# The last pair of token blocks as seven half-size products instead of eight, with its own order, its own bank for the last 128 tokens, and stores by column halves

## The chip, the cores and the metric

The kernel runs on one core of a Trainium2 chip. PE is the matrix engine (PEld its weight loads), DVE the vector engine, ACT the scalar engine, SP the engine that issues most of the DMAs; PSUM is the memory into which PE writes. The metric is the device time of one execution in microseconds (us). Most executions of one kernel lie within 0.4 us of each other; some take 1 to 2 us more. I therefore quote medians. For what happens at the end of the kernel I use a finer measure, the **tail**: the time from the start of the last hidden-layer eviction (the last ACT ReLU of 128x1024) to the end of the span. The start of the kernel, which varies from run to run, does not enter it. Times written like +10.21 are counted from that ReLU. Each tail is of the one execution of a kernel that was profiled.

## The reference

```python
def _attn_ref(x, f_logit, lower_bound):          # x: 4 x 6144 x 256
    sig = 1.0 / (1.0 + np.exp(-f_logit))
    f = lower_bound + (1.0 - lower_bound) * sig
    h = 0
    for t in range(S):                            # gated recurrence over the sequence
        h = f[:, t] * h + (1.0 - f[:, t]) * x[:, t]
        y[:, t] = h
    return y

def _moe_ref(x, w1, w2, w_out):                   # x: 24576 x 256, d_ff 1024
    g = np.maximum(x @ w1, x @ w2)
    return (g @ w_out).astype(np.float32)
```

## The kernel before

Tokens come in 48 blocks of 512. The kernel computes `max(h1, h2) = h1 + relu(h2 - h1)`, so that the second layer is `relu(y @ wd) @ w_out + y @ w13`: ten matmuls per 128 tokens, eight on hidden units and two on `y`. The hidden units and `y` are cut into two halves (`k` = 0, 1) and the 256 output columns too (`lo`, `hi`). Two blocks `ja`, `jb` make a pair, and for all pairs but some first ones and **the last** the second layer is done by a scheme of seven products instead of eight (`sevenths`). Sums of activations (`sum1` to `sum4`, on DVE) and of weights (`t1` to `t4`, made once) go in; PSUM banks X, E and B collect the products. The products of one pair run in the gaps of the next pair's first layer:

```python
        product("X", part(0, 0), plain(0, lo), True)   # M1
        then(seed("B", "X"))                           # ACT copies X into bank B
        product("E", sub(1), given(t1), True)          # M5
        then(snapshot("E", 5))                         # ACT copies E to SBUF
        product("X", sub(2), given(t2))                # M6
        then(snapshot("X", 2))
        product("B", part(0, 1), plain(1, lo))         # M2
        then(leave("B", ja, lo, None, False))          # ACT:  ja lo = B
        product("X", sub(3), given(t3))                # M7
        then(leave("X", jb, hi, 5, False))             # DVE:  jb hi = X + M5
        product("E", sub(4), plain(1, hi))             # M3
        then(leave("E", ja, hi, 2, True))              # DVE:  ja hi = E + (M1 + M6); store ja
        product("X", part(1, 1), given(t4))            # M4
        then(leave("X", jb, lo, None, True))           # ACT:  jb lo = X; store jb
```

Each product is 20 matmuls of 128x128 weights by 128 columns. The last pair has no next pair to hide behind, so it was done the plain way, with 40 matmuls of 256 columns per block, and the last block was evicted and stored in four quarters of 128 KB:

```python
        for step in queue:
            step()
        for j in (NBLK - 2, NBLK - 1):
            for slot in range(FC):
                second_layer(j, slot)
    # ... in second_layer:
            if j == NBLK - 1 and s == n - 1:
                (nc.vector.tensor_copy if r else nc.scalar.copy)(
                    out=osb[:, i : i + 1, :], in_=ps[:, r : r + 1, :]
                )
                store(j, osb, i, 1, nc.sync if r else nc.scalar)
```

Of the kernel before, what the change touches and what calls it, by code (L numbers as in the profile page):

```python
# [14 lines left out]
P = 128  # L15
# [3 lines left out]
def kernel(  # L19
# [429 lines left out]
                func=AF.Relu,  # L449
            )  # L450

    def store(j, osb, first=0, n=TB // P, queue=None):
        b, t0, nb, c, o = blocks[j]
        r0 = b * S + t0
        (queue or nc.sync).dma_start(
            out=out[r0 : r0 + nb, :].rearrange("(p n) d -> p n d", p=P)[
                :, first : first + n, :
            ],
            in_=osb[:, first : first + n, :],
        )  # L460

    acc = {}
# [1 line left out]
    def second_layer(j, slot):  # L464
        ns = TB // P
        n = KC + FC
        total = ns * n
        for k in range(slot * total // FC, (slot + 1) * total // FC):
            i, s = divmod(k, n)
            g, r = divmod(i, 2)  # L470
            if s == 0 and (r == 0 or j == NBLK - 1):
                acc["ps"] = ps_o.tile([P, 2, D], FP32, name="ps")
                if i == 0:
                    acc["osb"] = opool.tile([P, TB // P, D], FP32, name="osb")
            ps, osb = acc["ps"], acc["osb"]
            toks = slice(i * P, (i + 1) * P)
            if s < KC:
                left, right = y_of(j, s)[:, i:TB:ns], w13[:, s, :]
            else:
                fc = s - KC  # L480
                left, right = rts[j, fc // KH][:, fc % KH, toks], wob[:, fc, :]
            nc.tensor.matmul(  # L482
                ps[:, r, :],
                lhsT=left,
                rhs=right,
                start=(s == 0 and (r == 0 or j == NBLK - 1)),
                stop=(s == n - 1 and (r == 1 or j == NBLK - 1)),
                skip_group_check=True,
            )
            if j == NBLK - 1 and s == n - 1:  # L490
                (nc.vector.tensor_copy if r else nc.scalar.copy)(
                    out=osb[:, i : i + 1, :], in_=ps[:, r : r + 1, :]
                )
                store(j, osb, i, 1, nc.sync if r else nc.scalar)
            elif r == 1 and s == n - 1:
                (nc.scalar.copy if j == 0 else nc.vector.tensor_copy)(  # L496
                    out=osb[:, 2 * g : 2 * g + 2, :], in_=ps[:]
                )
                if i == ns - 1:
                    store(j, osb)  # L500
# [11 lines left out]
    def sum3(p):  # L512
        sum_of(p, 3, quarter(p, 0, 0), quarter(p, 1, 0), ALU.subtract)

    def sum2(p):
        sum_of(p, 2, quarter(p, 1, 1), sums[p, 3][:], ALU.subtract)

    def sum1(p):
        sum_of(p, 1, quarter(p, 1, 0), quarter(p, 1, 1), ALU.add)
# [4 lines left out]
    def sevenths(p):  # L524

        bank, snap, osbs = {}, {}, {}
        steps = []
        ja, jb = 2 * p, 2 * p + 1

        def product(b, left, w, fresh=False):  # L530
            for i in range(TB // P):
                for k in range(KH + 1):
                    steps.append([b, left, w(k), i, k, fresh and i == k == 0, None])

        def then(fn):
            steps[-1][-1] = fn

        def open_bank(b):
            bank[b] = ps_o.tile([P, TB // P, P], FP32, name="ps")

        def seed(b, src):
            def go():
                open_bank(b)
                nc.scalar.copy(out=bank[b][:], in_=bank[src][:])
            return go

        def snapshot(b, name):
            def go():
                t = snpool.tile([P, TB // P, P], FP32, name="sn")
                nc.scalar.copy(out=t[:], in_=bank[b][:])  # L550
                snap[name] = t
            return go

        def leave(b, j, cols, name, last):
            def go():
                if j not in osbs:
                    osbs[j] = opool.tile([P, TB // P, D], FP32, name="osb")
                dst = osbs[j][:, :, cols]
                if name is None:
                    nc.scalar.copy(out=dst, in_=bank[b][:])  # L560
                else:
                    nc.vector.tensor_tensor(  # L562
                        out=dst, in0=bank[b][:], in1=snap[name][:], op=ALU.add
                    )
                if last:
                    store(j, osbs[j])
            return go

        def sub(n):
            return lambda: sums[p, n]  # L570

        def part(t, k2):
            return lambda: rts[2 * p + t, k2]

        def plain(k2, cols):
            a, b = right(k2, cols)
            return lambda k: a[:, k, :] if k < KH else b

        def given(t):
            return lambda k: t[:, k, :]  # L580

        product("X", part(0, 0), plain(0, lo), True)
        then(seed("B", "X"))
        product("E", sub(1), given(t1), True)
        then(snapshot("E", 5))
        product("X", sub(2), given(t2))
        then(snapshot("X", 2))
        product("B", part(0, 1), plain(1, lo))
        then(leave("B", ja, lo, None, False))
        product("X", sub(3), given(t3))  # L590
        then(leave("X", jb, hi, 5, False))
        product("E", sub(4), plain(1, hi))
        then(leave("E", ja, hi, 2, True))
        product("X", part(1, 1), given(t4))
        then(leave("X", jb, lo, None, True))

        def runner(step):
            b, left, w, i, k, fresh, after = step

            def run():  # L600
                if fresh:
                    open_bank(b)
                a = left()
                cols = slice(i * P, (i + 1) * P) if k < KH else slice(i, TB, TB // P)
                nc.tensor.matmul(  # L605
                    bank[b][:, i, :],
                    lhsT=a[:, k, cols],
                    rhs=w,
                    start=fresh,
                    stop=after is not None,  # L610
                    skip_group_check=True,
                )
                if after is not None:
                    after()
            return run

        return [runner(s) for s in steps]

    with tc.manual_schedule():
# [93 lines left out]
        for p in range(PAIR0, NPAIR):  # L713
            first = p == PAIR0
            more = p + 1 < NPAIR
            seq = [(27, scans[p]["scan10"]), (36, scans[p]["scan11"])]
            if more:
                scans[p + 1] = pair_scans(p + 1)
                seq += [
                    (64, scans[p + 1]["decay0"]),  # L720
                    (66, scans[p + 1]["drive0"]),
                    (70, scans[p + 1]["scan00"]),
                    (84, scans[p + 1]["scan01"]),
                    (112, lambda: sum3(p)),
                    (131, scans[p + 1]["decay1"]),
                    (133, scans[p + 1]["drive1"]),
                ]
            if not first:
                seq += [
                    (9, lambda: sum1(p - 1)),  # L730
                    (18, lambda: sum2(p - 1)),
                    (50, lambda: sum4(p - 1)),
                ]
                queue += sevenths(p - 1)
            seq.sort(key=lambda e: e[0])
            gates = {4: 0, 6: 1, 12: 2, 14: 3} if more else {}
            for slot in range(2 * FC):
                first_layer(2 * p + slot // FC, slot % FC)
                if first and slot % 2:
                    second_layer(2 * p - 1, slot // 2)  # L740
                if p > PAIR0 + 1 or (p == PAIR0 + 1 and slot >= LAG):
                    due += NSEV / (2 * FC)
                    while due >= 1:
                        due -= 1
                        queue.pop(0)()
                if slot == 2 and p + 3 < NPAIR:
                    cross(blocks[2 * p + 6][3])
                if slot in gates:
                    pair_gate(p + 1, gates[slot])
                while seq and seq[0][0] < (slot + 1) * 9:  # L750
                    seq.pop(0)[1]()
        for step in queue:
            step()
        for j in (NBLK - 2, NBLK - 1):
            for slot in range(FC):
                second_layer(j, slot)


# [28 lines left out]
```

## Time and profile before

| kernel before | |
|---|---|
| time, median of 3 runs | 380.85 us (380.81 to 381.16) |
| span of the profiled run | 379.8 us |
| tail (last ReLU to end) | 14.37 us |
| last matmul ends | +10.21 |
| last eviction ends | +10.66 |
| last store issued / last packet done / landed | +10.69 / +12.04 / +12.60 |

The page of the kernel before, its span, the busy times and the clock that was granted to TensorE in 40 slices:

```profile
span 379.8 us, 9454 instructions
...
PE 369.1 (97%) x4076; PEld 279.9 (74%) x4076; DVE 333.0 (88%) x402; ACT 300.3 (79%) x406; POOL 37.5 (10%) x79
...
PEclk9999999999999999999999999999999999999999
```

PE is busy for 97% at the full clock; the body of the kernel is bound by it. The chain that ended last, before, in order of time, its last two pieces (start, length, what):

```profile
365.36 1.51 PE ps L605 x27
366.87 8.75 PE ps L482 x80
```

The chain leads through 80 matmuls of L482, the second layer of the last pair, 8.75 us. The timeline of the same stretch (start, length, engine, line, operation, result and operands, count, idle time before):

```profile
365.40 1.02 ACT L444 ACTIVATE r<-dT 128x1024 f16<-128x1024 f32 x1 [0.79 <-PE dT L436]
...
365.54 1.17 PEld L605 LDWEIGHTS <-r 128*128 128x128 f16 x20
...
366.65 8.67 PEld L482 LDWEIGHTS <-r 128*128 128x128 f16 x80
...
374.57 1.04 PE L482 MATMUL ps<-wob,r 128*128 128x256 f16 x8
...
375.64 0.42 DVE L491 COPY osb<-ps 128x256 f32<-128x256 f32 x1 [1.76 <-PE ps L482]
```

Here one reads the two cadences that the change trades: 80 weight loads and matmuls of 256 columns in 8.75 us, 109 ns each, and just before them 20 of 128 columns from 365.54 to 366.65, 55.5 ns each. Before its last copy DVE sat idle for 1.76 us, waiting for PE. The DMA view of the last 6.4 us before (373.4 to 379.8; one digit is 0.16 us, the mean busy share of the 16 DMA engines in tenths):

```profile
DMA  9999699249810008950000895000000000000100
...
out_dram<-osb SPq DMA_DIRECT2D x2, 128.0 KB, 1.9
out_dram<-osb ACTq DMA_DIRECT2D x1, 128.0 KB, 1.8
```

The last two stores land 1.8 to 1.9 us after their issue.

### The profile page before, as it was taken

To read this page: it belongs to the slowest core of one execution; us is meant where nothing else is said; L and a number is where in the kernel's file an instruction comes from. 1 tells how busy PE (TensorE), PEld (TensorE's weight loads), DVE (VectorE), ACT (ScalarE), POOL (GpSimd) and SP (SyncE) were. 2 spreads that over 40 slices of the span, in tenths; PEclk is the share of its full clock that TensorE was granted. 3 is DMA by queue.
4 is the path that set the end of the run, shared out by engine and by line. 5 is a ranking of instruction groups with operands and counts; after the bars stand their busy time and mean duration, and the time that the engine had idled before them with its cause. 6 is when DMAs were issued, how large, how long until landed. Compare 5 with 4: busy or idle time off the path is not lost.

```text
span 379.8 us, 9454 instructions
## 1 busy us (share of the span) xinstructions
PE 369.1 (97%) x4076; PEld 279.9 (74%) x4076; DVE 333.0 (88%) x402; ACT 300.3 (79%) x406; POOL 37.5 (10%) x79
## 2 busy tenths in 40 slices
PE   4999999999999999999999999999999999999995
PEld 3677766777777777777777777777777777777784
DVE  4696789999999999999999999999999999999721
ACT  4846788798798888888888887987888888888740
POOL 1500103101201101102011011011011021000000
PEclk9999999999999999999999999999999999999999
DMA  7994999989999999999899999999999999970223
GB/s 249 242 226 98 265 162 256 167 156 289 195 195 276 180 190 251 202 172 285 143 257 190 219 251 278 127 263 223 182 263 212 188 268 211 192 265 3 110 113 113
DMA packets 103389, 77.17 MB, mean 203 GB/s; under 512 B 93554, under 2 KB 94066, under 8 KB 102642
## 3 DMA queue, kind: packets, MB, share of 16 engines
q1 hardware_dynamic: 100514, 51.13, 59.8%
q0 software_dynamic: 2544, 25.17, 34.5%
q8 instruction: 32, 0.52, 0.6%
q10 hardware_dynamic: 288, 0.26, 0.2%
q14 instruction: 11, 0.09, 0.1%
HBM read 53.48 MB, written 48.23 MB: 268 GB/s over the span
## 4 chain that ended last, share of the span: by engine, by line
PE 89%; DMA 4%; DVE 3%; POOL 1%; SPq 1%; ACT 0%; issue 0%
PE ps L605 42%; PE dT L436 41%; PE ps L482 6%; DMA xT<-in_x_dram 3%; DMA r<-in_moe_w_dram 1%; DVE r L230 1%; DVE S L506 1%; SPq L117 0%; PE ps L180 0%; DVE osb L496 0%; DVE v L223 0%; POOL fT L105 0%; DVE ff L213 0%; ACT r L444 0%; POOL wob L631 0%
## 5 line engine op out<-in xcount | busy, mean ns | idle before, releaser
L444 ACT ACTIVATE r<-dT 128x1024 f16<-128x1024 f32 x192 | 195.8, 1022 | 53.2 <-PE dT L436 53.0
L436 PE MATMUL dT<-r,wd 128*128 128x512 f16 x768 | 225.4, 379 | 1.0 <-DVE wd L360 0.5
L605 PEld LDWEIGHTS <-S 128*128 128x128 f16 x1680 | 110.9, 101 | 37.6 <-issue 0.6
L605 PEld LDWEIGHTS <-r 128*128 128x128 f16 x1260 | 87.3, 101 | 36.6
L230 DVE TENSOR_TENSOR_SCAN r<-ff,r,v 128x512 f16<-128x512 f16 x88 | 108.2, 1270 | 0.8
L605 PE MATMUL ps<-t,S 128*128 128x128 f16 x1260 | 97.8, 219 | 0.0
L436 PEld LDWEIGHTS <-wd 128*128 128x128 f16 x768 | 67.6, 113 | 6.4 <-DVE wd L360 1.1
L506 DVE TENSOR_TENSOR S<-r 128x2560 f16<-128x2560 f16 x42 | 62.4, 1485 | 10.1 <-ACT r L444 10.0
L605 PE MATMUL ps<-wob,r 128*128 128x128 f16 x672 | 67.4, 219 | 0.0
L506 DVE TENSOR_TENSOR S<-r,S 128x2560 f16<-128x2560 f16 x42 | 61.9, 1474 | 0.0
L285 ACT ACTIVATE u<-fT 128x512 f16<-128x512 f16 x88 | 56.0, 636 | 1.0 <-DMA fT<-scr 1.0
L213 DVE TENSOR_SCALAR ff<-u,nom 128x512 f16<-128x512 f16 (+1 forms) x98 | 31.3, 346 | 9.7 <-ACT u L207 5.3
L348 POOL CAST waited<-fT 128x1 f32<-128x1 f16 x21 | 10.8, 513 | 279.5 <-DMA fT<-scr 279.5
L605 PE MATMUL ps<-w,r 128*128 128x128 f16 x168 | 36.8, 219 | 0.0
L562 DVE TENSOR_TENSOR osb<-ps,sn 128x512 f32<-128x512 f32 x42 | 28.7, 684 | 6.8 <-ACT osb L560 5.3
L605 PE MATMUL ps<-t,r 128*128 128x128 f16 x420 | 33.4, 219 | 0.0
L605 PE MATMUL ps<-wob,S 128*128 128x128 f16 x336 | 31.4, 219 | 0.0
L223 DVE TENSOR_TENSOR v<-u,xT 128x1024 f16<-128x1024 f16 x44 | 30.1, 684 | 0.2 <-DMA xT<-scr 0.2
L482 PEld LDWEIGHTS <-r 128*128 128x128 f16 x240 | 23.9, 101 | 6.9
L482 PE MATMUL ps<-wob,r 128*128 128x256 f16 x192 | 26.8, 273 | 0.0
L550 ACT COPY sn<-ps 128x512 f32<-128x512 f32 x42 | 24.6, 587 | 1.1 <-PE ps L605 0.9
L560 ACT COPY osb<-ps 128x512 f32<-128x512 f32 x42 | 24.4, 582 | 0.5 <-PE ps L605 0.5
(56 smaller groups left out, 134.8 us busy)
## 6 DMA issues: line engine op xcount, KB each, us to landing
out_dram<-osb SPq DMA_DIRECT2D x47, 512.0 KB, 3.9
scr<-in_f_logit_dram POOLq DMA_DIRECT2D x22, 512.0 KB, 7.4
scr<-in_x_dram POOLq DMA_DIRECT2D x22, 512.0 KB, 10.4
r<-in_moe_w_dram SPq DMA_DIRECT2D x4, 512.0 KB, 6.8
fT<-in_f_logit_dram POOLq DMA_DIRECT2D x3, 256.0 KB, 9.2
xT<-in_x_dram POOLq DMA_DIRECT2D x3, 256.0 KB, 11.1
osb<-in_f_logit_dram SPq DMA_DIRECT2D x2, 256.0 KB, 4.5
osb<-in_x_dram SPq DMA_DIRECT2D x2, 256.0 KB, 4.1
```

Of the source, the lines that this page charges most:

```text
L213: nc.vector.tensor_scalar(out=ff[:, h, cols], in0=u[:, h, cols], scalar1=nom[:, h : h + 1], scalar2=1.0, op0=ALU.mult, op1=ALU.add,)
L223: nc.vector.tensor_tensor(out=like(v[:, :, cols], xT), in0=like(u[:, :, cols], xT), in1=xT, op=ALU.mult,)
L230: nc.vector.tensor_tensor_scan(out=y_of(j, h), data0=ff[:, h, o : o + TB], data1=v[:, h, o : o + TB], initial=0.0 if t0 == 0 else y_of(j - ...
L285: nc.scalar.activation(out=mids[p + NBLK, "u"][:, h, cols], in_=held[c, 0][:, h, cols], func=AF.Sigmoid, scale=-1.0,)
L436: nc.tensor.matmul(dT[:, fc % 2, :], lhsT=wd[:, kc, unit_cols(fc)], rhs=y_of(j, kc), start=(kc == 0), stop=(kc == KC - 1),)
L444: nc.scalar.activation(out=rts[j, k][:, g - 1 : g + 1, :].rearrange("p q (i m) -> p q i m", m=P), in_=dT[:].rearrange("p q (m i) -> p q i ...
L482: nc.tensor.matmul(ps[:, r, :], lhsT=left, rhs=right, start=(s == 0 and (r == 0 or j == NBLK - 1)), stop=(s == n - 1 and (r == 1 or j == N ...
L506: nc.vector.tensor_tensor(out=t[:], in0=a, in1=b, op=op)
L550: nc.scalar.copy(out=t[:], in_=bank[b][:])
L560: nc.scalar.copy(out=dst, in_=bank[b][:])
L562: nc.vector.tensor_tensor(out=dst, in0=bank[b][:], in1=snap[name][:], op=ALU.add)
L605: nc.tensor.matmul(bank[b][:, i, :], lhsT=a[:, k, cols], rhs=w, start=fresh, stop=after is not None, skip_group_check=True,)
```

## The change

The intent: use the seven products for the last pair too. 140 matmuls of 128 columns replace 80 of 256, 7.77 us of PE instead of 8.75 at the cadences above. Since nothing hides the waits there, M2 is cut in two so that it fills two of them, and the last group of 128 tokens of M4 goes to a bank of its own, so that the rest can be evicted while it runs. The four quarters of the result (`ja lo`, `jb hi`, `ja hi`, `jb lo`) are stored each as soon as they are done, as column halves: runs of 512 B in DRAM. The core of the diff (cuts marked):

```diff
+        end = p == NPAIR - 1
@@ leave() @@
-                if last:
+                if end:
+                    store(j, osbs[j], cols=cols)
+                elif last:
                     store(j, osbs[j])
+        def leave_both(b):
+            def go():
+                leave(b, jb, hi, 5, False)()
+                t = snpool.tile([P, TB // P, P], FP32, name="sn")
+                nc.scalar.copy(out=t[:, 3, :], in_=bank[b][:, 3, :])
+                snap[4] = t
+            return go
+        def leave_last(at):                      # jb lo: groups 0-2 from X by ACT, group 3 from Y by DVE
+            ...
+                store(jb, osbs[jb], at, lo, nc.sync if at.start else nc.scalar)
@@ order of the products @@
+        if end:
+            product("B", part(0, 1), plain(1, lo), groups=range(1))
+            product("X", sub(2), given(t2))
+            then(snapshot("X", 2))
+            product("B", part(0, 1), plain(1, lo), groups=range(1, 4))
+            then(leave("B", ja, lo, None, False))
+            product("X", sub(3), given(t3))
+            then(leave_both("X"))
+            product("E", sub(4), plain(1, hi))
+            then(leave("E", ja, hi, 2, True))
+            product("X", part(1, 1), given(t4), groups=range(3))
+            then(leave_last(slice(0, 3)))
+            product("Y", part(1, 1), given(t4), True, groups=range(3, 4))
+            then(leave_last(slice(3, 4)))
@@ end of the kernel @@
-        for j in (NBLK - 2, NBLK - 1):
-            for slot in range(FC):
-                second_layer(j, slot)
+        p = NPAIR - 1
+        sum1(p)
+        sum2(p)
+        sum4(p)
+        for step in sevenths(p):
+            step()
... (cut: second_layer loses its special case for the last block; sum3 of the last pair moves into its first layer)
```

More of the change, by code (lines that the diff above doesn't have):

```diff
@@ L450, in first_layer, with store @@
             )
-    def store(j, osb, first=0, n=TB // P, queue=None):
+    def store(j, osb, groups=slice(0, TB // P), cols=slice(0, D), queue=None):
         b, t0, nb, c, o = blocks[j]
@@ L456, in store @@
             out=out[r0 : r0 + nb, :].rearrange("(p n) d -> p n d", p=P)[
-                :, first : first + n, :
+                :, groups, cols
             ],
-            in_=osb[:, first : first + n, :],
+            in_=osb[:, groups, cols],
         )
@@ L470, in second_layer @@
             g, r = divmod(i, 2)
-            if s == 0 and (r == 0 or j == NBLK - 1):
+            if s == 0 and r == 0:
                 acc["ps"] = ps_o.tile([P, 2, D], FP32, name="ps")
@@ L485, in second_layer @@
                 rhs=right,
-                start=(s == 0 and (r == 0 or j == NBLK - 1)),
-                stop=(s == n - 1 and (r == 1 or j == NBLK - 1)),
+                start=(s == 0 and r == 0),
+                stop=(s == n - 1 and r == 1),
                 skip_group_check=True,
             )
-            if j == NBLK - 1 and s == n - 1:
-                (nc.vector.tensor_copy if r else nc.scalar.copy)(
-                    out=osb[:, i : i + 1, :], in_=ps[:, r : r + 1, :]
-                )
-                store(j, osb, i, 1, nc.sync if r else nc.scalar)
-            elif r == 1 and s == n - 1:
+            if r == 1 and s == n - 1:
                 (nc.scalar.copy if j == 0 else nc.vector.tensor_copy)(
@@ L528, in sevenths, with product, open_bank @@
         ja, jb = 2 * p, 2 * p + 1
-        def product(b, left, w, fresh=False):
-            for i in range(TB // P):
+        end = p == NPAIR - 1
+        def product(b, left, w, fresh=False, groups=range(TB // P)):
+            for i in groups:
                 for k in range(KH + 1):
-                    steps.append([b, left, w(k), i, k, fresh and i == k == 0, None])
+                    new = fresh and i == groups[0] and k == 0
+                    steps.append([b, left, w(k), i, k, new, None])
         def then(fn):
             steps[-1][-1] = fn
-        def open_bank(b):
-            bank[b] = ps_o.tile([P, TB // P, P], FP32, name="ps")
+        def open_bank(b, i=0):
+            if i:
+                t = ps_d.tile([P, 2 * TB // P, P], FP32, name="dT")
+            else:
+                t = ps_o.tile([P, TB // P, P], FP32, name="ps")
+            bank[b] = t
         def seed(b, src):
@@ L564, in go @@
                     )
-                if last:
+                if end:
+                    store(j, osbs[j], cols=cols)
+                elif last:
                     store(j, osbs[j])
+            return go
[5 more added lines that the diff above has]
+                snap[4] = t
+            return go
+        def leave_last(at):
+            def go():
+                dst = osbs[jb][:, at, lo]
+                if at.start:
+                    nc.vector.tensor_tensor(
+                        out=dst, in0=bank["Y"][:, at, :], in1=snap[4][:, at, :],
+                        op=ALU.add,
+                    )
+                else:
+                    nc.scalar.copy(out=dst, in_=bank["X"][:, at, :])
+                store(jb, osbs[jb], at, lo, nc.sync if at.start else nc.scalar)
             return go
@@ L585, in sevenths @@
         then(snapshot("E", 5))
-        product("X", sub(2), given(t2))
-        then(snapshot("X", 2))
-        product("B", part(0, 1), plain(1, lo))
-        then(leave("B", ja, lo, None, False))
-        product("X", sub(3), given(t3))
-        then(leave("X", jb, hi, 5, False))
-        product("E", sub(4), plain(1, hi))
-        then(leave("E", ja, hi, 2, True))
-        product("X", part(1, 1), given(t4))
-        then(leave("X", jb, lo, None, True))
+        if end:
[12 more added lines that the diff above has]
+            then(leave_last(slice(3, 4)))
+        else:
+            product("X", sub(2), given(t2))
+            then(snapshot("X", 2))
+            product("B", part(0, 1), plain(1, lo))
+            then(leave("B", ja, lo, None, False))
+            product("X", sub(3), given(t3))
+            then(leave("X", jb, hi, 5, False))
+            product("E", sub(4), plain(1, hi))
+            then(leave("E", ja, hi, 2, True))
+            product("X", part(1, 1), given(t4))
+            then(leave("X", jb, lo, None, True))
         def runner(step):
@@ L601, in run @@
                 if fresh:
-                    open_bank(b)
+                    open_bank(b, i)
                 a = left()
@@ L715 @@
             more = p + 1 < NPAIR
-            seq = [(27, scans[p]["scan10"]), (36, scans[p]["scan11"])]
+            seq = [
+                (27, scans[p]["scan10"]),
+                (36, scans[p]["scan11"]),
+                (112, lambda: sum3(p)),
+            ]
             if more:
@@ L723 @@
                     (84, scans[p + 1]["scan01"]),
-                    (112, lambda: sum3(p)),
                     (131, scans[p + 1]["decay1"]),
```

## The prediction

> **What bounds it now.** The chain that ended last is 89% PE; the busy table gives PE 97% of a 379.8 us span, at full granted clock. The change touches only the last 14 us, so I read that stretch of the timeline. The last seven-product step of the pair before ends its issue at 366.65 us. Then 80 second-layer matmuls (128x256) run back to back for 8.75 us (the chain's last entry), 109 ns each, to 375.6. The last DVE copy (0.42 us) ends at 376.06, its 128 KB store is issued at 376.1, lands about 1.9 us later (DMA landing table), and about 1.8 us of ending follow. So PE and then one copy plus one store latency end the kernel; DVE and ACT are mostly idle there (1.5 to 4.9 us idle before each copy).
>
> **What changes.** Order of all engines: the body stays the same, except one more 1.48 us subtraction (sum3) on DVE in slot 12 of the last pair, where DVE has a 5.3 us gap: free. The tail's 80 matmuls of 256 columns become 140 of 128 columns. Such matmuls ran 20 in 1.11 us just before (timeline, 365.54 to 366.65), 55.5 ns each: 140 x 55.5 = 7.77 us. PE work saved: 0.98 us.
>
> **Added waits.** M5 needs sum1, which needs the last relu (ends 366.42) and the DVE add before it (ends 366.48). At 1.48 us sum1 is ready at about 367.96, while M1 ends at 367.76: PE idles 0.2 to 0.35 us. sum2 follows at about 369.4, just when M5 and the first quarter of M2 are done: wait 0 to 0.1. The rest of M2 (0.83 us) covers the 0.59 us snapshot of X before M7: 0 to 0.1. sum4 (about 370.8) is early for M3; M3 (1.1 us) covers the 0.69 us leaving of X before M4. PE should end at about 374.9 instead of 375.6: 0.7 us earlier.
>
> **After PE.** The last add is 128 columns, about 0.28 us (copies: 0.42 us for 256, 0.69 for 512), so it ends near 375.2, against 376.06: 0.85 us earlier. But the stores change from runs of 1 to 4 KB to runs of 512 B, and more bytes fall late: 256 KB (ja, high half) near 374.5, 192 KB near 375.1 and 64 KB near 375.4 to 375.5. An issue of 128 runs takes about 0.43 us on SP, of 256 runs 0.61 (the weights, four in 2.46), so 512 runs about 0.95 by estimate; the last store can queue behind it on SP. Data start about 0.9 us after issue. 512 KB at 300 to 390 GB/s (before's stores reached about 390) take 1.3 to 1.7 us from about 375.4, ending near 377.0, against 377.4 before. The Trainium skill (DMA: Bandwidth & Descriptors, Specifications) puts line rate at transfers of 512 B and more, so I expect no collapse; no run here shows 512 B stores yet. I therefore give half of the gain back: net about 0.45 us.
>
> **Prediction.** 380.4 us, 8 in 10 between 379.7 and 380.9. Faster by over 2%: 0.5%. Within 2%: 99%. Slower by over 2%: 0.5%.
>
> **What would show it.** Tail cadence about 55 ns per matmul; one PE gap of 0.2 to 0.35 us before M5, on the DVE sum, and almost none elsewhere; last matmul near 374.9; SP issue of a 512-run store near 0.95 us; last store landing 0.3 to 0.7 us earlier than before's 378.0; nothing moved before 366 us.
>
> **What would make it wrong.** Slow 512 B stores (landing over 3 us) or SP issue holding the last store: no gain or a small loss. Cheaper sums or no store backlog: the full 0.85 us. A stall at each sum (PE waiting on DVE three times) would eat the 0.98 us.

## The result

| | before | changed |
|---|---|---|
| time, median of 4 runs | 380.83 us (380.80 to 381.16) | 380.91 us (380.61 to 381.26) |
| ratio, 95% interval | | 1.0001 (0.9983 to 1.0018) |
| tail in the profile | 14.37 | 14.27 |
| last matmul ends | +10.21 | +9.67 |
| last eviction ends | +10.66 | +10.06 |
| last store issued | +10.69 | +10.10 |
| last DMA packet done | +12.04 | +12.28 |
| last landing | +12.60 | +12.70 |

All ratios in this document are the mean time of one kernel's fast runs over that of the kernel before in the same rounds, so they are not quite the ratio of the medians quoted. The time is the same; the tail is 0.10 us shorter. (The two spans differ by 1.0 us, 379.8 against 378.8, but 0.84 us of that is the start of the last ReLU, 365.40 against 364.56: this execution of before had started late. A second profile of before has its ReLU at 364.48.)

The page of the changed kernel:

```profile
span 378.8 us, 9587 instructions
...
PE 368.5 (97%) x4136; PEld 280.0 (74%) x4136; DVE 338.0 (89%) x405; ACT 303.0 (80%) x410; POOL 36.0 (10%) x79
...
PEclk9999999999999999999999999999999999999998
```

PE lost only 0.6 us of busy time; busy time is the wrong view here, since matmuls overlap (one of 128 columns lasts 0.22 us in the timeline, and one starts every 55.5 ns). The 8 at the end of the clock row lies after the last matmul (the granted clock is 1.00 up to 374.3 us and 0.71 in the rest) and costs nothing. The chain that ended last, in order of time:

```profile
364.52 2.64 PE ps L644 x47
367.17 5.76 PE ps L644 x100
372.95 1.00 PE ps L644 x15
```

The timeline of the tail of the changed kernel:

```profile
364.56 1.02 ACT L444 ACTIVATE r<-dT 128x1024 f16<-128x1024 f32 x1 [0.79 <-PE dT L436]
...
365.62 1.49 DVE L501 TENSOR_TENSOR S<-r 128x2560 f16<-128x2560 f16 x1
...
367.16 1.13 PEld L644 LDWEIGHTS <-S 128*128 128x128 f16 x20 [0.17 <-DVE S L501]
367.17 1.29 PE L644 MATMUL ps<-t,S 128*128 128x128 f16 x20
...
371.91 0.69 DVE L563 TENSOR_TENSOR osb<-ps,sn 128x512 f32<-128x512 f32 x1 [1.87 <-PE ps L644]
...
372.63 0.27 ACT L576 COPY sn<-ps 128x128 f32<-128x128 f32 x1 [1.27 <-DVE osb L563]
...
372.95 1.00 PE L644 MATMUL ps<-t,r 128*128 128x128 f16 x15
...
374.33 0.29 DVE L584 TENSOR_TENSOR osb<-dT,sn 128x128 f32<-128x128 f32 x1 [0.67 <-PE dT L644]
```

The chain breaks at the two waits of PE. Their length is read on the weight loads, because the matmuls still in flight hide most of it in the chain: 0.17 us before M5 (367.17), which waits for `sum1`, whose 1.49 us began when the ReLU was done; and 0.14 us before M4 (372.95). The second was not foreseen: the ACT copy of X's last group (L576) did not run beside the DVE addition (L563) that reads the same bank, it waited for it, and M4 waited for both (`plain_order` below has no such copy and no such wait). The Trainium skill (PSUM — Partial Sum Buffer, section "PSUM bank collisions raise a hardware error") says that two engines must not access one bank and quadrant at once, reads against reads included, and that a compiler's scheduler puts a dependency between them. The trace agrees with the serialisation: the copy begins 0.03 us after the addition ends. What would happen without the dependency, no run here shows.

The matmuls kept the cadence that was foreseen, and PE ends 0.54 us earlier. All of it, and the 0.06 us of the shorter last copy, arrives at the issue of the last store: +10.10 instead of +10.69. After that it is lost. The DMA view of the changed kernel's last 6.3 us (372.56 to 378.84):

```profile
DMA  0888887079989828999988888860000000000200
...
out_dram<-osb SPq DMA_DIRECT2D x2, 256.0 KB, 2.6
out_dram<-osb ACTq DMA_DIRECT2D x1, 192.0 KB, 2.8
out_dram<-osb SPq DMA_DIRECT2D x1, 64.0 KB, 2.4
```

The DMA engines are now busy almost without a pause for over 4 us, and the last stores take 2.4 and 2.8 us to land instead of 1.8 and 1.9.

### The profile page after: what moved, and what is told of

Its sections match the earlier page's. It is cut to its first block, busy times and chain, and to the rows that moved or that the text cites. A ratio compares the mean times of both kernels' runs of the same rounds, so it can differ in the third digit from the quotient of the medians.

```text
span 378.8 us, 9587 instructions
## 1 busy us (share of the span) xinstructions
PE 368.5 (97%) x4136; PEld 280.0 (74%) x4136; DVE 338.0 (89%) x405; ACT 303.0 (80%) x410; POOL 36.0 (10%) x79
## 4 chain that ended last, share of the span: by engine, by line
PE 91%; DVE 6%; DMA 1%; ACT 0%; issue 0%; SPq 0%; DVEq 0%
PE ps L644 45%; PE dT L436 41%; PE ps L482 4%; DVE r L230 1%; DVE S L501 1%; DMA osb<-in_f_logit_dram 1%; PE ps L180 1%; DVE wd L360 1%; DVE v L223 1%; DVE r L264 1%; DVE ff L213 0%; PE ps L392 0%; DVE osb L491 0%; ACT r L444 0%; DVE S L356 0%
## 5 line engine op out<-in xcount | busy, mean ns | idle before, releaser
L644 PEld LDWEIGHTS <-S 128*128 128x128 f16 x1760 | 115.4, 101 | 37.8 <-issue 0.6
L644 PEld LDWEIGHTS <-r 128*128 128x128 f16 x1320 | 90.9, 101 | 36.8
L644 PE MATMUL ps<-t,S 128*128 128x128 f16 x1320 | 101.6, 219 | 0.0
L501 DVE TENSOR_TENSOR S<-r 128x2560 f16<-128x2560 f16 x44 | 65.4, 1487 | 14.5 <-ACT r L444 14.4
L644 PE MATMUL ps<-wob,r 128*128 128x128 f16 x704 | 69.9, 219 | 0.0
L501 DVE TENSOR_TENSOR S<-r,S 128x2560 f16<-128x2560 f16 x44 | 65.0, 1478 | 0.0
L644 PE MATMUL ps<-w,r 128*128 128x128 f16 x176 | 38.5, 219 | 0.0
L563 DVE TENSOR_TENSOR osb<-ps,sn 128x512 f32<-128x512 f32 x44 | 30.1, 685 | 3.2 <-PE ps L644 3.2
L644 PE MATMUL ps<-wob,S 128*128 128x128 f16 x352 | 32.6, 219 | 0.0
L482 PEld LDWEIGHTS <-r 128*128 128x128 f16 x160 | 16.0, 101 | 6.2
L644 PE MATMUL ps<-w,S 128*128 128x128 f16 x88 | 19.3, 219 | 0.0
```

The lines of the kernel that those rows point to most:

```text
L482: nc.tensor.matmul(ps[:, r, :], lhsT=left, rhs=right, start=(s == 0 and r == 0), stop=(s == n - 1 and r == 1), skip_group_check=True,)
L501: nc.vector.tensor_tensor(out=t[:], in0=a, in1=b, op=op)
L563: nc.vector.tensor_tensor(out=dst, in0=bank[b][:], in1=snap[name][:], op=ALU.add)
L644: nc.tensor.matmul(bank[b][:, i, :], lhsT=a[:, k, cols], rhs=w, start=fresh, stop=after is not None, skip_group_check=True,)
```

## The experiments

My first theory (A) was that PE's gain is real and the stores give it back, by bytes that come late and queue (A1) or by the slower start of stores with many short runs (A2). Rivals were chance, a latency of 512 B writes, and a fixed cost at the end. This table has all runs; "place" is explained in the third group, "What comes after the last landing". The repeat of the changed kernel and the three `drop_hi`, `drop_lo`, `only_last` were one set of runs, `joined` to `after_plus7` a second, the rest a third, each set on its own chip; each ratio is taken within its set.

| run | median us | ratio to before (95%) | tail | last packet | end after it | place of the last store |
|---|---|---|---|---|---|---|
| before, again | 380.73 | 1.0002 (0.9982 to 1.0022) | 14.37 | +12.04 | 2.33 | 1st |
| changed, again | 380.56 | 0.9999 (0.9986 to 1.0012) | 14.26 | +12.28 | 1.98 | 1st (192 KB: 8th) |
| drop_hi (wrong result) | 379.99 | 0.9986 (0.9972 to 1.0000) | 13.63 | +11.94 | 1.69 | 8th (192 KB: 7th) |
| drop_lo (wrong result) | 380.70 | 1.0009 (0.9986 to 1.0032) | 14.07 | +12.30 | 1.77 | 8th (192 KB: 7th) |
| only_last (wrong result) | 379.46 | 0.9971 (0.9959 to 0.9984) | 13.03 | +11.28 | 1.75 | 7th |
| joined | 381.49 | 1.0016 (1.0004 to 1.0028) | 14.71 | +12.83 | 1.88 | 7th |
| ja_whole | 380.80 | 1.0001 (0.9988 to 1.0014) | 14.53 | +12.68 | 1.85 | 8th (192 KB: 7th) |
| before_plus7 | 379.94 | 0.9989 (0.9974 to 1.0005) | 13.59 | +12.04 | 1.55 | 8th |
| after_plus7 | 380.25 | 0.9994 (0.9981 to 1.0007) | 13.99 | +12.61 | 1.38 | 8th (192 KB: 7th) |
| plain_order | 380.35 | 0.9980 (0.9967 to 0.9992) | 14.01 | +12.64 | 1.37 | 8th |
| halves | 379.50 | 0.9956 (0.9942 to 0.9970) | 13.23 | +11.91 | 1.32 | 8th |
| halves_plus1 | 380.71 | 0.9991 (0.9976 to 1.0007) | 13.98 | +11.91 | 2.07 | 1st |

### Does the tail repeat?

Both kernels unchanged, with new profiles.

> The changed kernel again, unchanged: does the tail repeat? I call tail the time from the start of the last ReLU (ACT, 128x1024) to the end of the span: 14.37 us in the profile of before, 14.27 in that of the changed kernel, while their bodies up to that point differed by 0.84 us (365.40 against 364.56) for nothing the change did. Theory A (stores gave back what PE gained): tail 14.2 to 14.4 again, last issue of a store at +10.1, last landing at +12.7. Rival B (chance of one profile): the tail moves by several tenths. Time ratio to before 0.999 to 1.001.

> The kernel before, unchanged, with a profile of its own: is 14.37 us from the last ReLU to the end its usual tail, although its first profile had a late start? Expected: tail 14.3 to 14.4, last landing at +12.6, end 1.77 us after it (last store on the first semaphore of the row). Time ratio to before 0.999 to 1.001.

Measured: tails of 14.26 and 14.37, within 0.01 us of the first profiles; PE ends at +9.66 and +10.20. In these repeats the tail resolves hundredths, where the medians of the time resolve two tenths at best; one later profile (`after_plus7`) did stray by 0.3 us. Chance of one profile is out as the explanation of these two tails.

### What of the loss is queueing? Stores left out

`drop_hi`: 256 KB, the last big store before the end, are not stored.

```diff
                 if end:
-                    store(j, osbs[j], cols=cols)
+                    if not last:
+                        store(j, osbs[j], cols=cols)
```

> Wrong on purpose: the 256 KB store of the first block's high columns, the last big one before the end, is left out; everything else stays. Theory A1 (the final 192 KB and 64 KB queue on the 16 DMA engines behind that store's 512 packets of 26.5 ns per engine group): the 192 KB store's data take about 0.6 us instead of 1.10, last landing from +12.70 to about +12.3 to +12.45, tail down by 0.25 to 0.4 us. Theory A2 (the loss is only the longer start of stores with many 512 B runs, 1.24 us against 0.84 from issue to first packet, which does not depend on other stores): landing and tail unchanged within 0.1 us.

`drop_lo`: the first of the late stores is left out (`if name is not None:` in the same place).

> Wrong on purpose: the 256 KB store of the first block's low columns, the first of the four late ones (issued at +6.83), is left out. If the late stores are one unbroken stream that began at +8.13 and was already full (theory A3, bandwidth of the whole tail), taking 1.05 us out of its front ends it 0.5 us or more earlier. If each store only waits for its own start and overlaps its neighbour a little (A1), nothing changes: last landing +12.7, tail within 0.1 us of the changed kernel's.

`only_last`: as `drop_hi`, and the 192 KB of L589 are not stored either; the last store is the 64 KB alone.

```diff
-                store(jb, osbs[jb], at, lo, nc.sync if at.start else nc.scalar)
+                if at.start:
+                    store(jb, osbs[jb], at, lo)
```

> Wrong on purpose: of the last three stores only the last, 64 KB in 128 runs of 512 B, is kept (no high columns of the first block, no 192 KB). If the PE side gained and only the stores gave it back (theory A), the last store behaves like before's last one: issue at +10.1, first packet 0.84 us later, landing 1.8 to 1.9 us after issue at about +12.0, tail about 13.5 to 13.7: 0.6 to 0.8 us below the changed kernel and below before. If 512 B writes have a longer latency of their own (rival), it still lands 2.4 us or more after issue, at +12.5, and the tail stays near 14.1.

Measured: leaving out the store in front moves the last landing from +12.69 to +12.29 (foreseen +12.3 to +12.45), as A1 has it and A2 has not. A1's way there was not quite right: the 192 KB store's data did not take 0.6 us instead of 1.10, but 1.05 (+10.89 to +11.94); they started 0.29 us earlier. Leaving out the earlier one moves nothing (+12.73): the late stores are not one long full stream from +8.13 on, only neighbours disturb each other. With both neighbours gone, the same last store lands 1.59 us after its issue instead of 2.44, and the kernel is 1.1 us faster than the changed one (379.46 against 380.56; of the 1.23 us in the tail, 1.00 lies before the last packet, the rest in what follows it). The latency of the 192 KB store in `drop_hi`, against the 2.8 us above:

```profile
out_dram<-osb ACTq DMA_DIRECT2D x1, 192.0 KB, 2.4
```

The DMA view of `only_last` in its last 5 us (372.58 to 377.62, 0.13 us a digit) shows the store of 64 KB alone, the digits 493:

```profile
DMA  0799999940798888930000049300000000000010
```

So the 0.6 us that PE and the last copy gained are there up to the issue of the last store, and its neighbours' bytes take them. A latency peculiar to 512 B writes is refuted.

Two numbers did not fit. The tail of `drop_hi` fell by 0.63 us although its last landing came only 0.40 us earlier, and that of `drop_lo` fell by 0.19 us although nothing landed earlier. The end came 1.98 us after the last packet in the changed kernel, but 1.69 and 1.77 in these. I had not asked what stands between the last landing and the end.

### What comes after the last landing

In the events of SP after the last store the trace has a row of waits, one for each of eight semaphores (counters) that the DMAs of SP and ACT take in turn. These are the events of the kernel before, with the start and end of each from the last ReLU, and the semaphores:

```
SP   DMA_DIRECT2D       +10.69..+11.03   the last store; it uses semaphore 100
SP   EVENT_SEMAPHORE    +12.61..+12.64   waits 100, 113
SP   EVENT_SEMAPHORE    +12.68..+12.71   waits 101, 112
SP   EVENT_SEMAPHORE    +12.74..+12.77   waits 102, 111
...                                      (103, 104, 105 and 106, 0.07 to 0.09 us each)
SP   EVENT_SEMAPHORE    +13.42..+13.45   waits 107, 118     (0.37 us after the one before it)
SP   DRAIN              +13.50..+13.55
```

(The second profile of before has the same times within 0.01 us.) The row has a fixed order. If the last store to land uses the first semaphore, all seven others are waited for after it, although they were complete long ago: 0.8 us, of which one step takes 0.37 us. (That step falls before or after the landing by the run: in `drop_hi` and `only_last` it came after it, in `before_plus7` before it.) If it uses the last one, the row has been gone through before. In these runs each DMA of SP or ACT that was added or removed turned the round by one. In the changed kernel the 192 KB store that lands last (+12.70) has the eighth place, but the 64 KB store (+12.54) has the first, so the row starts there.

`before_plus7` and `after_plus7`: seven loads of 64 B that nobody reads, in the middle of the kernel, to turn the round by seven.

```diff
+    extra = const.tile([1, 8, 16], FP32)
...
+                if slot == 9 and PAIR0 < p <= PAIR0 + 7:
+                    nc.sync.dma_start(
+                        out=extra[:, p - PAIR0 - 1, :],
+                        in_=lower_bound[16 * (p - PAIR0) : 16 * (p - PAIR0 + 1)]
+                        .rearrange("(o d) -> o d", o=1),
+                    )
```

> The kernel before, with seven 64 B loads added in the middle of the kernel, on the SP queue, read by nobody. At the end SP waits for the eight semaphores of the DMAs one after another, in a fixed order; before's last store has the first of them, so seven more waits and one step of 0.37 us come after its landing: 1.77 us from landing to the end, against 1.34 us in the two runs whose last store had one of the last semaphores. Seven more DMAs move the last store to the last semaphore of the row. Theory E (the row of waits is on the critical path): last landing still at +12.6, end 1.30 to 1.40 us later, tail 13.90 to 14.0 instead of 14.37, time about 0.4 us below before (ratio 0.999). Rival: what follows the landing is a fixed ending; tail 14.3 to 14.4.

> The changed kernel with the same seven loads. There the last store to land (192 KB, +12.70) has the last semaphore, but the 64 KB store, landing at +12.54, has the first, and the row of waits runs from there: end 1.57 us after the last landing. With seven more, both have the last two. Theory E: landings unchanged (+12.54 and +12.70), end 1.34 us after, tail 14.0 to 14.07 instead of 14.27. Rival (fixed ending): 14.25 to 14.3.

Measured: the kernel before **with seven useless loads more** is 0.8 us faster (380.72 to 379.94 in the medians; the tail goes from 14.37 to 13.59), and its last packet is done at the same +12.04. I had expected 0.4 us; the gain is twice that, because the step of 0.37 us, too, now falls before the landing. The waits of SP's queue, before and then with the seven loads, show the same store being waited for and less after it (what waited, for what, us in total, times, longest):

```profile
SPq L782 <- DMA out_dram<-osb: 1.5, 1, 1.5
SPq L782 <- PEq L782: 0.7, 2, 0.5
```

```profile
SPq L789 <- DMA out_dram<-osb: 0.8, 1, 0.8
SPq L789 <- PEq L789: 0.7, 2, 0.5
```

In the first the wait for the store ends and the row follows. In the second SP has done the row and waits for the store at its end, 0.8 us, and nothing but the common ending follows. The changed kernel gains 0.3 us by it (380.56 to 380.25), since only a part of its row was exposed; the tail of 13.99 comes from an execution whose last packets were late by 0.3 us (+12.61), so it says less. A fixed ending is refuted by the kernel before, and again below. It follows that the comparison of the two kernels mixed two things. At the favourable place both are faster, and by the medians the kernel before is then ahead (379.94 against 380.25). The intervals of both ratios still include 1, because each set holds executions that started late (381.14 and 381.65 us for `before_plus7`); the verdict rests on the tail, the unchanged last packet, and the medians.

### Longer runs instead of early halves

`joined`: the first block is stored whole, in runs of 4 KB, when its second half is done, and the last block as whole rows (3 groups, then 1).

```diff
-                if end:
-                    store(j, osbs[j], cols=cols)
-                elif last:
+                if last:
                     store(j, osbs[j])
@@ leave_last @@
-                store(jb, osbs[jb], at, lo, nc.sync if at.start else nc.scalar)
+                store(jb, osbs[jb], at, slice(0, D), nc.sync if at.start else nc.scalar)
```

> The changed kernel with its five late stores made into three with long runs: the first block whole (4 KB runs) when its high half is done, the second block as whole rows for 3 groups (3 KB runs) and 1 group (1 KB runs) at the end. If the short runs are the loss (theory A2): the store of 3 groups starts 0.84 us after its issue at +9.94 instead of 1.24, its 384 KB take about 1 us, last landing about +12.3, 0.4 us earlier than the changed kernel. If the amount of bytes left for the last moment is the loss (A1): 1024 KB have to go after +9.97 at about 400 GB/s, 2.6 us, so data end about +12.6 and the last landing comes at +13.0 to +13.1, 0.3 to 0.4 us later. Time within 0.2% of before in either case.

`ja_whole`: only the first block's halves are joined (`if end and j == jb:` in the same place).

> The changed kernel with only the first block's two half stores joined into one of 4 KB runs, issued when the second half is done (+9.1). A1 (bytes late): 512 KB instead of 256 KB are issued at +9.13 but run at 400 instead of 309 GB/s, so the last data end within 0.15 us of +12.28 and the last landing is within 0.15 us of +12.70. A2 (runs): fewer descriptors ahead of it let the 192 KB store start earlier and land about 0.3 us earlier. Besides, it has one DMA fewer, so the last store's semaphore comes last in the row of waits at the end (theory E, see the two runs with extra loads): ending after the last landing about 1.35 us, tail about 14.05 to 14.15.

Measured: `joined` lands at +13.04 and +13.29, later by 0.35 to 0.6 us (A1 had foreseen +13.0 to +13.1), and is slower than before (ratio 1.0016, the interval excludes 1): late bytes decide, not the number of runs alone. The DMA view of its last 6.7 us (373.54 to 380.25): idle, then 1 MB without a gap.

```profile
DMA  0000000000039999999999899998200000000010
```

`ja_whole` missed what I expected of both theories: its last landing came at +13.17, 0.5 us later, not within 0.15 us. The packets say why. The 192 KB store on ACT's queue, issued at +9.93, had its first packet at +11.59, in the very moment in which the 512 KB store ahead of it began to finish (+11.59). The same is true in `joined` (+11.29 and +11.30) and in the changed kernel (+11.18 and +11.18), and already in the kernel before, for the ACT store behind a 512 KB one (+8.71 and +8.70). Without a store just ahead (`drop_hi`) the same store started 0.96 us after its issue. So in these runs a large store just ahead on the other queue held the next one up until it began to finish. Why the two queues did not share the engines from the start is not settled. The Trainium skill (DMA: Bandwidth & Descriptors, section "Queues, rings and completion order") describes the engines as taking turns between queues packet by packet, but a packet there is a group of typically 9 to 17 descriptors (at most 64), not one run, as the profile counts them. The 512 KB store has 128 runs, so about 8 for each of 16 engines by estimate. If these were one such packet, the long wait would be no contradiction. The 64 KB store did run beside the 192 KB one (+11.52 to +12.18 within +11.18 to +12.28), which fits such turns too. No run here tests it.

### The refinements of the order

`plain_order`: the last pair in the order of all other pairs; no part of M2 before M6, all of M4 in X.

```diff
-            product("B", part(0, 1), plain(1, lo), groups=range(1))
             product("X", sub(2), given(t2))
             then(snapshot("X", 2))
-            product("B", part(0, 1), plain(1, lo), groups=range(1, 4))
+            product("B", part(0, 1), plain(1, lo))
             ...
-            then(leave_both("X"))
+            then(leave("X", jb, hi, 5, False))
             ...
-            product("X", part(1, 1), given(t4), groups=range(3))
-            then(leave_last(slice(0, 3)))
-            product("Y", part(1, 1), given(t4), True, groups=range(3, 4))
-            then(leave_last(slice(3, 4)))
+            product("X", part(1, 1), given(t4))
+            then(leave("X", jb, lo, None, True))
```

> The changed kernel without its two refinements: the last pair runs the seven products in the order of all other pairs (M2 whole after M6, M4 whole in X's bank), its four quarters still stored as halves of 512 B runs. Cost of that on PE and after: about 0.3 us more waiting for the second sum, 0.14 us less before M4, the last copy 0.58 instead of 0.29 us for 512 columns, the last store 256 KB instead of 64: last landing at about +12.95 instead of +12.70, 0.25 us later. But it has one DMA fewer, so its last store sits on the last semaphore of the row: by theory E the end follows 0.9 us after the landing instead of 1.57: tail 13.8 to 14.0, 0.3 to 0.45 us SHORTER than the changed kernel's 14.27, and time about 380.2. If the refinements are worth what they save before the stores and the ending is fixed (rival): tail 14.5, time 380.8.

Measured: PE waits 0.27 us for `sum2` but no longer before M4, and ends at +9.76 instead of +9.66; the last store lands at +13.08 instead of +12.69. Up to there the refinements are worth 0.39 us. Still the version without them has a tail of 14.01 against 14.26, because it has one store fewer and its last store takes the eighth place: the end comes 0.93 us after the landing instead of 1.57. It is also faster than before by the clock (0.9980, interval below 1; in medians 380.35 against 380.73 for the repeat of before in the same set, since several executions of before in that set took over 381 us). The refinements were good, and their extra DMA cost more than they earned.

### A version made from the findings

`halves` cuts each product of the last pair into two halves of the tokens with banks of their own (XA, XB, EA, EB, BA, BB), 10 matmuls each, interleaved so that each wait has another half product to hide it. Rows are stored whole, in four stores of 256 KB with 128 runs of 2 KB, the first two at +7.27 and +8.30. The order:

```python
half("X","A", M1); half("X","B", M1); half("E","A", M5); half("E","B", M5)
half("B","A", M2)   # ACT: ja lo, groups 0-1
half("X","A", M6);  half("B","B", M2)
half("X","A", M7)   # DVE: jb hi, groups 0-1
half("E","A", M3)   # DVE: ja hi, groups 0-1; store ja, groups 0-1
half("X","B", M6)
half("X","A", M4)   # ACT: jb lo, groups 0-1; store jb, groups 0-1
half("X","B", M7);  half("E","B", M3)   # store ja, groups 2-3
half("X","B", M4)   # store jb, groups 2-3
```

> A version built from the findings: the seven products of the last pair are each cut into two halves of the tokens (70 + 70 matmuls, X, E and B in two banks each), interleaved so that every sum, snapshot and leaving copy has another product to hide behind; rows are stored whole, four stores of 256 KB in 128 runs of 2 KB, the first two of them around +7.2 and +8.2. No DMA more than 256 KB waits at the end. Expected: PE gaps 0.2 us before the first product that needs a sum and at most 0.2 us before the last; last store issued at +10.0, first packet 0.84 us later, data about 0.65 us, last landing at about +12.1 (changed kernel +12.70, before +12.60); the last store is on the last semaphore, so the end comes about 0.9 us later: tail 13.0 to 13.1, time about 379.3 to 379.6, about 0.3% below before and 0.15% below before with seven more loads. If late bytes and runs do not matter as theory A1 says, the tail stays near 13.6.

`halves_plus1` is the same with one of the 64 B loads.

> The same version with one 64 B load more in the middle of the kernel, read by nobody: it turns the round of semaphores by one, so the last store sits on the first semaphore of the row, as before's does. Theory E: landing unchanged at +12.1, the end 1.7 to 1.8 us after it instead of 0.9: tail 13.8 to 13.9, 0.7 to 0.85 us longer than without the load. A fixed ending (rival): same tail within 0.1 us.

Measured: `halves` is correct and takes 379.50 us, ratio 0.9956, the fastest correct kernel here (0.997 by the medians, against 380.73 of the repeat of before in the same set). PE ends at +9.79, later than in the changed kernel (gaps of 0.17 and 0.15 us; the last eviction is 0.37 us), and yet its last store lands at +12.30 instead of +12.69. I had expected +12.1: the last store was issued at +10.23, 0.2 us later than estimated. The DMA view of its last 5.2 us (372.5 to 377.74):

```profile
DMA  1898982029999810008899999898712000000000
...
out_dram<-osb SPq DMA_DIRECT2D x3, 256.0 KB, 2.0
```

Stores of 256 KB now land in 2.0 us, where those of 512 B runs took 2.6, and there are gaps between the first three of them. With one load of 64 B more the last packet is done at the same +11.91, and the tail is 0.75 us longer (13.98). SP's waits for DMAs, in `halves` and then with the load more, show it too:

```profile
SPq L855 <- DMA out_dram<-osb: 0.9, 2, 0.7
```

```profile
SPq L862 <- DMA out_dram<-osb: 1.6, 1, 1.6
```

In the second the row comes after the wait. The profiled executions differ by 0.81 us (379.52 and 380.33), almost all of it tail; the median of the time is 1.2 us longer (380.71), and the rest of that is not explained. The effect of the row is thus shown on two kernels, in both directions and with the last packet unmoved; the medians of the changed kernel agree.

These runs also part the gain of `halves` over the kernel before, 1.14 us of tail, into its two causes. With the last store in the eighth place the tails are 13.23 (`halves`) and 13.59 (`before_plus7`), in the first place 13.98 and 14.37. The seven products with the new order and stores are worth 0.36 to 0.39 us; the other 0.75 to 0.78 us is the place, which the kernel before gets by seven useless loads.

## Why the prediction was right or wrong

The class was right (the same within 2%), and 380.91 us lies at the upper edge of the range, 379.7 to 380.9. That is no proof of the mechanism: "no change" (380.83) lay inside the range as well. The gain of 0.45 us did not come: the ratio is 1.0001, and the tail shows 0.10 us.

- *What bounds it:* right. The chain and the cadences (109 and 55.5 ns) held, and nothing moved before the last ReLU.
- *Added waits:* the first was right in kind and a little too large (0.2 to 0.35 us foreseen, 0.17 measured); "almost none elsewhere" missed the 0.14 us before M4, where ACT waited for DVE on the same bank. PE ended 0.54 us earlier, not 0.7.
- *The last add:* 0.29 us (foreseen 0.28), but it ended 0.60 us earlier than before's, not 0.85. Of the missing 0.25 us, 0.16 was lost on PE; the other 0.09 lies between the last matmul and the end of the add, 0.39 us where 0.3 was foreseen.
- *SP's issue:* an issue of 512 runs took 0.53 to 0.66 us, not 0.95, and did not hold the last store.
- **The step that failed** is the sum of the stores: "Data start about 0.9 us after issue. 512 KB at 300 to 390 GB/s … take 1.3 to 1.7 us from about 375.4, ending near 377.0, against 377.4 before". In the tail's time that is +11.6 against +12.0. Measured: the last packet was done at +12.28. The data of the 256 KB store started near +10.3, 1.2 us after its issue instead of 0.9, and the 512 KB took 2.0 us (+10.3 to +12.28), which is about 266 GB/s. One packet of 512 B took 26.5 ns on its engine, one of 4 KB in the tail of the kernel before 164 ns (means): per byte 77% of the rate. I had named the queueing, mis-sized it by 0.7 us, and so gave back half of the gain where all of it went.
- *What was missing altogether:* the row of waits after the last landing, 0.9 to 1.8 us by the place of the last store. I had taken the "about 1.8 us of ending" over unchanged. In the changed kernel the end came 0.35 us sooner after the last packet (1.98 against 2.33 us); 0.20 us of this lies after the last landing (1.57 against 1.77), the rest between the packet and the landing. This is why the tail came out 0.10 us shorter although the last packet was done 0.24 us later. That was luck: nothing in the prediction provided for it.

Not settled: why one step in the row takes about 0.37 us and what decides where in the row it falls, and the rule by which a later store waits for an earlier one on the other queue.

## What to carry to other kernels

At the end of a kernel, ask what the last store finds on the DMA engines: here half a megabyte issued in the last microsecond cost more than the 0.6 us that compute saved, so let the big, long-run stores go early and keep the end free. Look at what follows the last landing too, because one small load in the middle of the kernel changed it here by 0.75 us, and a comparison of two variants with a different number of DMAs is not one of the change alone. Where effects are that small, compare from a fixed late event in the trace, not whole times.

## What the Trainium skill lacked or had wrong

- DMA: Bandwidth & Descriptors, section "Specifications", gives 512 B as the size from which a transfer runs at line rate. Stores with runs of 512 B moved at 77% of the rate per engine of those with 4 KB (26.5 ns for 512 B, 45.6 for 1 KB, 84 for 2 KB, 164 for 4 KB, means of the packets in the tails).
- The same page does not say how the start depends on the number of runs when SP issues. From issue to first packet on idle engines: 0.83 us with 128 runs, 1.30 us with 512 (of which SP's issue itself took 0.33 and 0.65 us).
- The same page, section "Queues, rings and completion order", gives typically 9 to 17 descriptors as one turn, but not how the runs of a store from SP or ACT are put together into turns. In three runs the later store's first packet came only when the earlier store began to finish (+11.18, +11.29 and +11.59). Whether this is against the page was not tested.
- I found no page that has the row of waits on the DMA semaphores at the end: it is in fixed order, 0.07 us a step and one step of 0.37 us, and the place of the last store in it, with that step, was worth 0.78 us (tail 14.37 against 13.59). Runtime: NRT & Kernel Launch, section "The ~15µs preamble/postamble breakdown", lists after the kernel a barrier of about 1.5 us, a reset of semaphores and a re-arming of the DMA rings, but no such row.
- PSUM — Partial Sum Buffer, on readers of one bank, agrees with what was seen: ACT's copy began 0.03 us after DVE's addition ended.
